# First loads in another order, DRAM stores as operations of their own and a new order of the first eight units, in a Strassen kernel of six cross layers

## The chip, the cores and the metric

The kernel runs on one core of one Trainium2 chip. The metric is the time of one execution on the device in microseconds (us), given as the median of several runs. The profile's own span is shorter than the time (2279.1 us beside 2280.82 us for the run that was profiled). All runs quoted here are fast: no run was more than 1.5% above the fastest of its kernel.

Short names: PE is the matrix engine, PEld its weight loads, DVE the vector engine, ACT the scalar engine, POOL the engine that issues the stores to DRAM here, and SP the engine that issues nearly all the loads. SBUF is the on-chip memory and a PSUM bank a matmul accumulator.

## The reference

```python
B, F, D, L = 16384, 100, 16, 6
Din = min(F * D, 1024)                     # 1024
# x0: (B, Din), ws: (L, Din, Din), bs: (L, Din), all bf16

def reference(x0, ws, bs):
    x = x0
    for l in range(ws.shape[0]):
        proj = jnp.einsum('bd,de->be', x, ws[l]) + bs[l]
        x = x0 * proj + x
    return x
```

Each layer is a matmul of 16384 x 1024 by 1024 x 1024, then a multiply by x0 and an add.

## The kernel before

A *unit* is one layer for one *pair* of 512-row blocks: 16 pairs times 6 layers make 96 units of about 24 us. x is held transposed, features on the partitions, in quadrants: `B11`, `B12`, `B21`, `B22` are (feature half, row half). Each unit's product is made by Strassen's scheme (Winograd's form). DVE makes four sums of x (`T1` to `T4`) and four sums of weight quadrants (combinations 5, 6, 7 and 3), and PE makes seven products `P1` to `P7` instead of eight. From the second pair on, products 5 and 2 are split once more. They need eight more sums of weights (`2i` and `5i`, four quarters each) and six more sums of x (`2t13, 2t2, 2t4, 5t13, 5t2, 5t4`).

Names in the profiles: `wp` are weight quadrants and their sums, in a ring of 16 tiles that are used in turn; `w` is the quadrant w12 (1, w12, 2 and 4 are the four quadrants of a layer's weights); `isum` are the sums 2i and 5i; `x0T` is x0 and `xst` the running x; `T` and `ti` are sums of x; `ev` are products on their way out of PSUM; `Lc` is the DRAM store of the weight sums; `pA` and `pX` are PSUM banks.

The weight sums depend only on the layer. So the first six units make them and *store* them to DRAM (`Lc`), and later units load them. This first pass, about 145 us long, is the only part that the change touches in substance.

```python
isum = [work.tile([P, KH, H], BF16, name=f"isum{i}") for i in range(4)]   # two layers' sums: layer l and l + 2 share
...
def combo(name, w, a, b, o_, deps, u=u, raw=raw):
    def fn():
        t = ring_make(u, w)
        tt(t[:], raw(a)[:], raw(b)[:], o_)                                # DVE
        nc.gpsimd.dma_start(Lc[units[u][1], CIDX[w]]..., t[:])            # its store, at once
    add(name, fn, ...)
...
for X, s in (("2i", isum[2 * (l % 2)]), ("5i", isum[2 * (l % 2) + 1])):
    def icombo(i, fn, rd, wr, ...):       # one quarter; it names only its own quarter
        add(X + i, fn, [f"{X}{l % 2}.{r}" for r in rd] + ..., [f"{X}{l % 2}.{wr}"], [X[0]])
    def save(X=X, s=s, l=l):
        nc.gpsimd.dma_start(Lc[l, CIDX[X]], s[:]...)                      # all four quarters
    icombo("5", ...); icombo("6", ...)
    # "3" and "7" follow; the one that is last by a fixed rule calls save()
```

The order of each engine's instructions is fixed when the program is built. Every operation has a rank (a time in us, relative to its unit's start), a heap takes the lowest rank among the operations whose predecessors are out, and each engine then runs its own in that order. The first eight units have rank tables of their own:

```python
EARLY = [ranks("""P1.3@-.68 P1.1@.19 ... 2i5@-7.88 ... c5@4.62 T1@5.76 ..."""),     # unit 0
 ...
 ranks("""... 2t13@-62.26 2t2@-10.85 T1@-9.38 2t4@-8.25 ...""")]                    # unit 6: second pair, layer 0
...
ttop(X + "t13", t_[:, 0:2], ..., SUB, [src], [X + "t13"])   # "2t13" reads B21, which in unit 6 is x0 of the second pair
ttop(X + "t2", t_[:, 2], q(1, 1), t_[:, 0], SUB, [src, X + "t13"], [X + "t2"])
```

The x0 of the second pair is loaded by two transposing loads (one for each 512 rows), issued in unit 2:

```python
if l == (2 if pr == 0 else 0) and nxt < NPAIR:
    for n in range(2):
        XN = [f"x0.{nxt % 2}.{d}{n}" for d in range(2)]
        def ld(n=n, nxt=nxt):
            nc.sync.dma_start_transpose(out=x0Ts[nxt % 2][:, n], in_=x0[nxt * PR + n * NB:..., :])
        op(base + 23 + n, ld, [], XN)
```

The first loads of all:

```python
for w in ("1", "2"):
    nc.scalar.dma_start(wt[(0, w)][:], w_src(0, w))
nc.scalar.dma_start(b_rows[:], bs...)                  # 12 KB of biases
load_half(nc.scalar, "w12", 0); load_half(nc.scalar, "4", 0)
load_quarter(0, 0); load_quarter(1, 0); load_quarter(0, 1)       # transposing loads of x0, SP
load_half(nc.sync, "w12", 1); load_half(nc.sync, "4", 1)
load_quarter(1, 1)
```

## Time and profile before

| what | value | where it is read |
|---|---|---|
| time | 2281.74 us, 3 runs, 2279.78 to 2283.31 | runs |
| PE busy | 99% of the span | page, part 1 |
| PE on the chain of work that ended last | 96% | page, part 4 |
| 16 matmuls of 128x512 without a gap | 3.45 us (216 ns each) | starts in PE's timeline |
| first real matmul | 9.20 us | PE's timeline |
| idle time of PE after it | 3.7 us in all | PE's waits |

All waits of PE in the kernel before (engine, tile, line, what it waited for: us in total, times, longest):

```profile
PE pX L558 <- DMA b_rows<-in_bs_dram: 3.3, 1, 3.3
PE pX L284 <- DVE T L197: 2.6, 2, 1.5
PE pX L531 <- DVE zeros L528: 1.2, 1, 1.2
PE pX L284 <- DVE wp L197: 0.9, 1, 0.9
PE pX L396 <- DVE ti L197: 0.2, 1, 0.2
```

L284 is the plain matmul, L396 the one of the second split, L197 the helper behind nearly every DVE operation. L558 is a small matmul that transposes the biases, so the first real matmul waits 3.3 us for them (the first quarter of x0, which it needs as well, landed only at 8.95 us). After that there is next to nothing to gain in 2270 us.

### The profile page before, as it was taken

To read this page: it belongs to the slowest core of one execution; us is meant where nothing else is said; L and a number is where in the kernel's file an instruction comes from. 1 tells how busy PE (TensorE), PEld (TensorE's weight loads), DVE (VectorE), ACT (ScalarE), POOL (GpSimd) and SP (SyncE) were. 2 spreads that over 40 slices of the span, in tenths; PEclk is the share of its full clock that TensorE was granted. 3 is DMA by queue.
4 is the path that set the end of the run, shared out by engine and by line. 5 is a ranking of instruction groups with operands and counts; after the bars stand their busy time and mean duration, and the time that the engine had idled before them with its cause. 6 is when DMAs were issued, how large, how long until landed. Compare 5 with 4: busy or idle time off the path is not lost.

```text
span 2279.1 us, 34736 instructions
## 1 busy us (share of the span) xinstructions
PE 2252.4 (99%) x12713; PEld 1263.8 (55%) x12951; DVE 2079.8 (91%) x2326; ACT 1841.2 (81%) x3228; POOL 20.0 (1%) x42
## 2 busy tenths in 40 slices
PE   8999999999999999999999999999999999999998
PEld 3455555555555555555555555555555555555554
DVE  6999999999999999999999999999999999999997
ACT  5678888878888888888888888888888888888887
POOL 1110000000000000000000000000000000000000
PEclk9999999999999999999999999999999999999999
DMA  9869797796977969779697796978969689696872
GB/s 276 241 232 291 271 252 266 211 311 196 247 263 215 302 212 250 258 225 283 215 263 250 226 282 214 262 252 226 284 204 285 233 230 284 195 293 227 240 241 66
DMA packets 625868, 557.01 MB, mean 244 GB/s; under 512 B 397600, under 2 KB 552224, under 8 KB 625696
## 3 DMA queue, kind: packets, MB, share of 16 engines
q1 hardware_dynamic: 617808, 534.05, 79.1%
q0 software_dynamic: 5184, 18.88, 2.1%
q10 hardware_dynamic: 2704, 1.85, 0.3%
q8 instruction: 101, 1.65, 0.3%
q14 instruction: 71, 0.58, 0.1%
HBM read 436.22 MB, written 52.43 MB: 214 GB/s over the span
## 4 chain that ended last, share of the span: by engine, by line
PE 96%; DVE 1%; SPq 1%; issue 1%; DMA 1%; ACT 0%; DVEq 0%; ACTq 0%
PE pA L284 56%; PE pX L396 24%; PE pX L284 16%; DVE ev L197 1%; SPq L534 1%; DMA w<-in_ws_dram 1%; DVE xst L197 0%; ACT ev L293 0%; DVE T L197 0%; DVE isum L197 0%; SPq L547 0%; SPq L245 0%; DVE wp L197 0%; DVE x0T L494 0%; ACT pX L289 0%
## 5 line engine op out<-in xcount | busy, mean ns | idle before, releaser
L284 PEld LDWEIGHTS <-wp 128*128 128x128 bf16 x7904 | 772.3, 98 | 843.0 <-issue 2.9
L284 PE MATMUL pA<-T,wp 128*128 128x512 bf16 x4471 | 1048.6, 379 | 7.2
L293 ACT ACTIVATE ev<-pA,b_all 128x512 bf16<-128x512 f32 x1124 | 706.2, 691 | 212.1 <-PE pA L284 166.3
L396 PEld LDWEIGHTS <-wp 128*128 128x128 bf16 x4984 | 487.0, 98 | 158.3 <-issue 16.1
L197 DVE TENSOR_TENSOR ev<-ev,x0T 128x2048 bf16<-128x2048 bf16 (+2 forms) x484 | 483.2, 1000 | 7.9 <-ACT ev L293 1.3
L197 DVE TENSOR_TENSOR xst<-ev,xst 128x2048 bf16<-128x2048 bf16 x319 | 389.2, 1220 | 18.8 <-DVE ev L197 0.5
L396 PE MATMUL pX<-ti,wp 128*128 128x256 bf16 x2848 | 397.9, 272 | 0.2 <-DVE ti L197 0.2
L197 DVE TENSOR_TENSOR ev<-ev,ev 128x2048 bf16<-128x2048 bf16 (+1 forms) x283 | 343.9, 1215 | 25.5 <-ACT ev L293 7.4
L293 ACT ACTIVATE ev<-pX,b_all 128x512 bf16<-128x512 f32 x412 | 288.9, 706 | 61.4 <-PE pX L284 51.3
L284 PE MATMUL pX<-xst,wp 128*128 128x512 bf16 x1369 | 335.8, 379 | 0.3
L284 PE MATMUL pA<-xst,wp 128*128 128x512 bf16 x1205 | 302.3, 379 | 4.0
L289 ACT COPY pX<-pA 128x512 f32<-128x512 f32 x412 | 256.7, 627 | 39.9 <-PE pA L284 39.9
L289 ACT CAST ev<-pX 128x512 bf16<-128x512 f32 x384 | 225.1, 620 | 52.2 <-ACT ev L293 37.3
L197 DVE TENSOR_TENSOR ev<-iu,ip 128x1024 bf16<-128x1024 bf16 x178 | 122.6, 689 | 120.5 <-ACT iu L289 120.4
L289 ACT COPY pX<-pX 128x512 f32<-128x512 f32 x356 | 208.7, 587 | 8.3
L289 ACT CAST iu<-pX 128x512 bf16<-128x512 f32 x356 | 197.1, 639 | 1.0 <-PE pX L396 0.9
L197 DVE TENSOR_TENSOR T<-xst 128x2048 bf16<-128x2048 bf16 x160 | 194.9, 1218 | 0.3
L197 DVE TENSOR_TENSOR T<-xst,T 128x2048 bf16<-128x2048 bf16 x160 | 194.8, 1218 | 0.2
L396 PE MATMUL pX<-T,wp 128*128 128x256 bf16 x1068 | 160.2, 273 | 0.0
L289 ACT CAST ip<-pX 128x512 bf16<-128x512 f32 x178 | 104.8, 589 | 53.7 <-PE pX L396 53.7
L396 PE MATMUL pX<-xst,wp 128*128 128x256 bf16 x888 | 133.2, 273 | 0.0
L197 DVE TENSOR_TENSOR xst<-ev,x0T 128x2048 bf16<-128x2048 bf16 x64 | 78.3, 1223 | 1.5
(44 smaller groups left out, 621.2 us busy)
## 6 DMA issues: line engine op xcount, KB each, us to landing
wp<-Lc SPq DMA_DIRECT2D x538, 512.0 KB, 4.6
wp<-in_ws_dram SPq DMA_DIRECT2D x285, 512.0 KB, 5.4
out_dram<-x0T SPq DMA_DIRECT2D x30, 1024.0 KB, 8.4
Lc<-wp POOLq DMA_DIRECT2D x24, 512.0 KB, 6.2
Lc<-isum POOLq DMA_DIRECT2D x12, 512.0 KB, 5.5
w<-in_ws_dram SPq DMA_DIRECT2D x5, 512.0 KB, 9.3
wp<-in_ws_dram ACTq DMA_DIRECT2D x2, 512.0 KB, 5.3
out_dram<-x0T SPq DMA_DIRECT2D x2, 512.0 KB, 3.4
```

The source lines that it names most:

```text
L197: nc.vector.tensor_tensor(out=o, in0=a, in1=b, op=op)
L284: nc.tensor.matmul(bank[:], lhsT=wt[(u, w)][:, k, m * P:(m + 1) * P], rhs=rhs[:, k, :], start=(start and k == 0), stop=(k == KH - 1), skip ...
L289: add(name, lambda: nc.scalar.copy(out=dst, in_=src), rd, wr)
L293: add(name, lambda: nc.scalar.activation(out=dst, in_=src, func=IDENT, bias=b_all[:, c:c + 1], scale=1.0), rd, wr)
L396: nc.tensor.matmul(pX[bank][:, m * NQ:(m + 1) * NQ], lhsT=wv[:, k, m * P:(m + 1) * P], rhs=rhs[:, k, :], start=(start and m == 0 and k == ...
L534: nc.sync.dma_start_transpose(out=blk(x0Ts[0], dh, n), in_=x0[n * NB:(n + 1) * NB, dh * H:(dh + 1) * H])
```

## The change

The change does three things. As I read its intent, the first is to start the first unit sooner, the second is to let the scheduler know about the stores, and the third is to refit the order to both.

1. The biases go first on ACT's queue, and the half loads of w12 and 4 all go to SP.
2. A store is an operation of its own, which reads all that it stores. The next writer of the tile has to wait for it.
3. All the rank tables of the first eight units are new.

```diff
+SAVES = ranks("s5@16 s6@17 s7@18 s3@20 s2i@21 s5i@22")
 EARLY = [ranks("""
   ... every table replaced; the two entries that matter below: ...
-2t13@-62.26 2t2@-10.85 T1@-9.38 2t4@-8.25 ...            (unit 6)
+2t13@-153.59 2t2@-151.71 2t4@-29.05 T1@-9.32 ...
-2i5@-14.20 c5@-6.78 ...                                  (unit 4)
+2i5@-22.08 c5@-7.99 T1@5.10 ...
@@
+            def save(w, t, rd, weights=(), l=l):
+                def fn():
+                    nc.gpsimd.dma_start(Lc[l, CIDX[w]]..., t()[:])
+                add("s" + w, fn, rd, (), weights)
@@ combo: ring_make, DVE operation; the store leaves it
+                save(w, lambda raw=raw, w=w: raw(w), [f"w{u}.{w}"], [w])
@@ icombo: the four quarters, in any order that their own inputs allow; f3/f7 with their save() leave
+                save(X, lambda s=s: s, [rn(i) for i in "5637"])
@@ first loads
+    nc.scalar.dma_start(b_rows[:], ...)
     for w in ("1", "2"):
         nc.scalar.dma_start(wt[(0, w)][:], w_src(0, w))
-    nc.scalar.dma_start(b_rows[:], ...)
-    load_half(nc.scalar, "w12", 0)
-    load_half(nc.scalar, "4", 0)
     load_quarter(0, 0)
     load_quarter(1, 0)
     load_quarter(0, 1)
-    load_half(nc.sync, "w12", 1)
-    load_half(nc.sync, "4", 1)
+    for h in range(2):
+        load_half("w12", h)
+        load_half("4", h)
     load_quarter(1, 1)
```

(Cut: the other ranks, the bank of the bias matmul, and plain rewriting.)

**What the second point mends.** In the kernel before, the store of unit 0's `5i` comes with the quarter that the fixed rule calls last, `5i7`, ranked at 54.56 us. Unit 2 shares the tile. Its first quarter, `5i5`, has rank 3.42 in a unit that starts at 48.4, so it is at 51.8, and it names only that one quarter. The order of the built program shows that it is indeed overwritten first (place on the engine, line, operation):

```
DVE  57 L197 TensorTensor isum_102<-wp 128x512      unit 2's 5i5 writes quarter "5" of the tile
DVE  60 L197 TensorTensor isum_102<-wp 128x512      unit 0's 5i7, the last quarter of layer 0
POOL 17 L331 DMACopy Lc<-isum_102 128x2048          the store of layer 0's 5i, after DVE 60
```

The same happens between units 2 and 4. So the kernel before stores a wrong quarter in the `5i` of layers 0 and 2, and passes its comparison with the reference all the same (why it passes was not tested; a wrong x0 in run `e12` below was caught with a relative error of 0.35). The change is thus a correction as well.

## The prediction

> What bounds the kernel now. The matrix engine (PE): busy 2252.4 of 2279.1 us (99%) on the page, and 96% of the chain of waits that ended last. Busy is not rate, so I read starts: four matmuls of 128x512 take 0.86 us, sixteen 3.45 us. From the first real matmul (9.20 us) to the last (2273.2 us) that pace is left at few places only. The list of waits of PE has 1.2 + 3.3 us before the first real matmul, and after it DVE T 2.6 us in two pieces (1.15 us at 17.54, 1.48 us at 44.48), DVE wp 0.9 us at 19.52, DVE ti 0.2 us at 183.57. The change keeps all matmuls and vector work, so it can win at most these 3.7 us and part of the 9 us lead-in.
>
> The pieces of the change.
> 1. First loads. The 12 KB of biases go first on ACT's queue; the four half loads of w12 and 4 all go on SP's queue, after three transposing loads of x0. Before, the first matmul waited for the biases (landed 9.03 us), but the first quarter of x0 landed only at 8.95 us. So that wins 0.1 us. ACT's queue took about 106% of the 16 DMA engines between 8 and 10 us, and the transposes moved 0.05 MB there against 0.48 MB in the next 2 us (DMA view by window). That agrees with the Trainium skill, "DMA: Bandwidth & Descriptors", section "Issuing engines are not separate DMA queues": all queues interleave on the same engines. With the halves gone from there the second and third quarter should land 1 to 2 us earlier (12.64 and 16.17 before), so T1 comes earlier; but the first half of combination 5 comes later (11.3 before, about 16 to 17 after) and becomes the wait of P5. The fourth quarter, which T2 and P6 need, still comes last (20.64 before), and P6 began at 22.12, right after T2. The first unit therefore wins only about 0.4 us.
> 2. Saves as operations. The store of 2i (512 KB, 11.4 to 16.1 us, beside the transposes) moves behind those of 5, 6, 7, 3. The vector engine idled 2.36 us before combination 5 of unit 1, for a w12 that landed at 31.63 us; PE then waited 1.48 us for T1 of unit 1 (43.21 us). After, that chain is about 10.3 us from combination 5 to T1 (before 11.5 us) and w12 should land up to 1 us earlier. About 1.2 us of the 1.48 go away.
> 3. A tile whose save is not issued cannot be reused. Ring and sums have slack. I expect queue waits of SP, no wait of PE.
> 4. New order in units 2 to 7: the vector engine is busy 19 of 20 us there, PE already without gaps: nothing to win, up to a microsecond to lose.
>
> Sum: 0.4 + 1.2 + 0.2 - 0.2 = about 1.6 us. Predicted 2280.1 us, 2276.5 to 2283.5. Within 2%: 98%; faster 1%, slower 1%.
>
> What shows it: PE's wait for T near 44 us shorter than 0.5 us; waits in 16 to 23 us of 1 to 2 us, named combination 5 or T2; w12 of unit 1 landing before 31 us; the first real matmul at 8.5 to 9.2 us; 93 matmuls of 128x512 in 20 us from 60 us on; the page's PE busy time within 3 us of before.
>
> What would make it wrong: the fourth quarter landing well after 21 us, so that P6 waits over 1 us; a save waiting behind an unfinished one on POOL's in-order queue, holding a ring tile so long that unit 3 to 6 lacks weights; a vector order that makes PE wait at a unit's start.

## More of the kernel before

The head of the page of the kernel before:

```profile
span 2279.1 us, 34736 instructions
PE 2252.4 (99%) x12713; PEld 1263.8 (55%) x12951; DVE 2079.8 (91%) x2326; ACT 1841.2 (81%) x3228; POOL 20.0 (1%) x42
```

The trace of this run lacks 238 matmul records: 12713 beside 12951 weight loads, of which there is one for each matmul. PE's busy time can therefore not be compared between two kernels. I compare the starts of the weight loads, which are complete.

What DVE does around 95 us, in unit 3 (start, length, engine, line, operation, out<-in; a bracket would show idle time before it):

```profile
94.78 1.22 DVE L197 TENSOR_TENSOR wp<-wp,w 128x2048 bf16<-128x2048 bf16 x1
...
96.25 0.68 DVE L197 TENSOR_TENSOR ti<-x0T 128x1024 bf16<-128x1024 bf16 x1
96.86 1.22 DVE L197 TENSOR_TENSOR T<-xst 128x2048 bf16<-128x2048 bf16 x1
```

The second line is `2t13` of unit 6, 50 us ahead of its use, put into unit 3. It reads the first 512 rows of the second pair's x0. Their load was issued at 74.06 us and landed 18.3 us later, at 92.37 us (issues of DMA in the window of 72 to 76 us, last number: us from issue to landing):

```profile
x0T<-in_x_dram SPq DMA_TRANSPOSE x1, 18.3
```

So here the load was in 3.9 us before DVE came to its reader. Nobody waited, and no view lists a wait that did not happen.

## The result and the profile after

| kernel | median | runs | ratio to before |
|---|---|---|---|
| before | 2281.14 us | 4, 2279.78 to 2283.31 | |
| changed | 2287.35 us | 4, 2285.37 to 2289.91 | 1.0027, 95% interval 1.001 to 1.0044 |

A ratio is the mean time of one kernel's fast runs over that of the other's fast runs of the same rounds, so it is not quite the ratio of the medians. The change is 0.27% slower, which counts as "same" at 2%, but all four runs lie above the predicted range of 2276.5 to 2283.5 us. The profiled run was the slowest of the four: its span is 9.07 us longer than before's, while the medians differ by 6.2 us.

The head of the page after:

```profile
span 2288.1 us, 34970 instructions
PE 2267.6 (99%) x12951; PEld 1264.2 (55%) x12951; DVE 2080.4 (91%) x2326; ACT 1842.7 (81%) x3228; POOL 19.8 (1%) x42
```

DVE, ACT and PEld do the same work in the same time (here all matmul records are there, so PE's number is no growth). The page alone says nothing. PE's waits after:

```profile
PE pX L286 <- DVE xst L199: 8.3, 2, 7.2
PE pX L286 <- DMA x0T<-in_x_dram: 1.5, 1, 1.5
PE pX L286 <- DVE T L199: 1.3, 1, 1.3
PE pX L518 <- DVE zeros L515: 1.2, 1, 1.2
PE pA L286 <- DMA x0T<-in_x_dram: 0.8, 1, 0.8
...
```

The wait for the biases is gone, and one wait of 7.2 us is new. To see when time was won and lost, I compare the start of the weight load at the same place in PE's order with that of before (us; negative is ahead; my own table from the two traces):

| place (time of before) | 9.2 us | 24 us | 49 us | 86 us | 98 us | 122 us | 580 us | end of span |
|---|---|---|---|---|---|---|---|---|
| changed kernel | -2.38 | -1.88 | -0.83 | -0.83 | +8.54 | +8.54 | +8.31 | +9.07 |

The better start is real (2.4 us at the first real matmul), most of it is gone by 49 us, and one step of 9.37 us between 86 and 98 us makes the whole loss. It is never made up again, as PE has no slack.

DVE's timeline at the step:

```profile
83.42 0.69 DVE L199 TENSOR_TENSOR ev<-ev,x0T 128x1024 bf16<-128x1024 bf16 x1
93.15 0.69 DVE L199 TENSOR_TENSOR ti<-x0T 128x1024 bf16<-128x1024 bf16 x1 [9.04 <-DMA x0T<-in_x_dram]
93.88 0.42 DVE L199 TENSOR_TENSOR ti<-x0T,ti 128x512 bf16<-128x512 bf16 x1
94.22 0.42 DVE L199 TENSOR_TENSOR isum<-wp 128x512 bf16<-128x512 bf16 x1
94.55 1.22 DVE L199 TENSOR_TENSOR xst<-ev,xst 128x2048 bf16<-128x2048 bf16 x1
```

The second line is the same `2t13`. In the new order it has place 78 among DVE's operations instead of 92 (counted from 0), and `2t2`, the other early sum of this x0, has place 79 instead of 144. DVE reaches it at 84.1 us, and its x0 lands only at 93.13 us. DVE runs in order, so everything behind it waits 9.04 us too, among it the `xst` of the fifth line, which has nothing to do with it and which PE needs. The Trainium skill, "TensorE: Matmul & The Clock Gate", section "Architectural detail: the array is 16× 32×32, not 1× 128×128", gives VectorE's queue as strictly first in, first out; this trace agrees, with 9.04 us of idle time and ready work behind it.

The chain of work that ended last, from 84 to 104 us, ties it together (start, length, what). Before, it consists of PE there:

```profile
85.92 3.62 PE pA L284 x16
89.54 6.04 PE pX L284 x28
```

and after, of the load and its readers:

```profile
72.47 20.66 DMA x0T<-in_x_dram
...
93.15 0.70 DVE ti L199
...
94.64 1.14 DVE xst L199
...
95.92 8.20 PE pX L286 x28
```

The wait of PE alone is not the whole step. Windows of before and after (stretch, its length, busy time and count of PE, PEld, DVE, ACT, POOL, then PE's granted clock, the DMA engines' share, GB/s):

```profile
88.50:95.90 7.40, 7.40 (x36) 3.38 (x35) 7.26 (x8) 5.16 (x9) 0.00 (x0) 1.00 1.20 235
95.90:100.00 4.10, 4.05 (x20) 1.86 (x20) 4.10 (x7) 2.54 (x5) 0.53 (x1) 1.00 0.94 198
```

```profile
88.50:95.90 7.40, 0.20 (x1) 0.01 (x1) 2.72 (x5) 0.69 (x2) 0.00 (x0) 0.81 1.10 216
95.90:100.00 4.10, 4.08 (x10) 1.49 (x11) 4.04 (x5) 1.16 (x2) 1.06 (x2) 0.51 0.95 256
```

After the wait PE starts only 10 matmuls in 4.1 us instead of 20, at a granted clock of 0.51. Ten matmuls start 427 ns apart instead of 216 ns, which is 2.1 us. So 7.2 + 2.1 = 9.3 us, the step. The Trainium skill, "TensorE: Matmul & The Clock Gate", section "What's actually happening", says that the clock falls to half after an idle window of about 3.4 us and comes back after as much busy time, with a window that runs freely. The trace agrees: the clock's record goes to half at 93.09 us, 4.4 us after PE ran out of work, and stays there for 6.83 us, about two such windows. In `e2` below a shorter wait was enough; see the last section.

Where did the lead of the start go before that? PE's timeline after:

```profile
6.83 2.75 PE L286 MATMUL pA<-x0T,wp 128*128 128x512 bf16 x12 [0.77 <-DMA x0T<-in_x_dram]
...
11.11 1.89 PE L286 MATMUL pX<-x0T,wp 128*128 128x512 bf16 x8 [1.53 <-DMA x0T<-in_x_dram]
...
38.74 3.61 PE L286 MATMUL pX<-xst,wp 128*128 128x512 bf16 x16 [1.08 <-DVE xst L199]
43.64 2.76 PE L286 MATMUL pX<-T,wp 128*128 128x512 bf16 x12 [1.28 <-DVE T L199]
```

PE begins 2.4 us sooner and then waits 1.5 us for the next quarter of x0, and in unit 1 1.1 us and 1.3 us for DVE. In unit 1 DVE itself is held up by a load. Before:

```profile
31.73 1.23 DVE L197 TENSOR_TENSOR wp<-w,wp 128x2048 bf16<-128x2048 bf16 x1 [2.36 <-DMA w<-in_ws_dram]
```

and after:

```profile
31.50 1.23 DVE L199 TENSOR_TENSOR wp<-w,wp 128x2048 bf16<-128x2048 bf16 x1 [3.50 <-DMA w<-in_ws_dram]
```

This is combination 5 of unit 1, which needs w12. It comes 0.2 us earlier than before, although DVE was free 1.4 us earlier: w12 landed at 31.41 us instead of 31.63 us. The lead ran into a load that had not moved.

### The profile page after: what moved, and what is told of

It is laid out like the page before. It is cut to its first block, busy times and chain, and to the rows that moved or that the text cites. A ratio compares the mean times of both kernels' runs of the same rounds, so it can differ in the third digit from the quotient of the medians.

```text
span 2288.1 us, 34970 instructions
## 1 busy us (share of the span) xinstructions
PE 2267.6 (99%) x12951; PEld 1264.2 (55%) x12951; DVE 2080.4 (91%) x2326; ACT 1842.7 (81%) x3228; POOL 19.8 (1%) x42
## 3 DMA queue, kind: packets, MB, share of 16 engines
q8 instruction: 101, 1.65, 0.3%
## 4 chain that ended last, share of the span: by engine, by line
PE 96%; DMA 1%; DVE 1%; SPq 1%; issue 0%; ACT 0%; DVEq 0%
PE pA L286 56%; PE pX L383 24%; PE pX L286 16%; DMA x0T<-in_x_dram 1%; DVE ev L199 1%; SPq L521 1%; DMA w<-in_ws_dram 1%; DVE xst L199 0%; DVE wp L199 0%; DVE T L199 0%; SPq L530 0%; SPq L247 0%; ACT ev L295 0%; DVE isum L199 0%; DVE x0T L481 0%
## 5 line engine op out<-in xcount | busy, mean ns | idle before, releaser
L286 PE MATMUL pA<-xst,wp 128*128 128x512 bf16 x1280 | 313.5, 379 | 0.0
```

What stands on the lines that cost most here:

```text
L286: nc.tensor.matmul(bank[:], lhsT=wt[(u, w)][:, k, m * P:(m + 1) * P], rhs=rhs[:, k, :], start=(start and k == 0), stop=(k == KH - 1), skip ...
```

## The experiments

The runs are called `e1` to `e14` after the first part of their labels. Theory A: the early place of `2t13` makes the loss, since DVE then waits for the x0 load. Rival B: the stores that are now waited for make it. Rival C: the new first loads make it. Fourteen runs took these apart. "Before" in the tables is the kernel before, run in the same rounds on the same chip.

### Only the two early sums of x put back (e1)

In the changed kernel, two ranks only:

```diff
-2t13@-153.59 2t2@-151.71 2t4@-29.05 T1@-9.32
+2t13@-62.26 2t2@-10.85 2t4@-29.05 T1@-9.32
```

> The changed kernel, but the two vector operations 2t13 and 2t2 of unit 6 (the only ones of the early units that read x0 of the second pair of blocks) go back to the ranks they had before, -62.26 and -10.85. Theory A: the change lost its time in one place, the 9.04 us that the in-order vector engine stood before 2t13 for the second x0 (landed at 93.13 us), which gave PE 7.2 us without work (88.5 to 95.9) and then 2.1 us at half clock (10 matmuls at 427 ns instead of 216). Then this run is at 2287.35 - 9.4 = about 2278 to 2280.5 us, below the kernel before by 0.5 to 3 us, no PE wait over 1 us between 60 and 120 us, PE clock 1.00 in 80 to 100 us. Rival B, the saves as operations made the loads and reuse of tiles late: the wait stays and the time stays at about 2287. Rival C, the rest of the new order is worse as well: the wait goes, but the time stays above 2282.

Measured: median 2282.44 us beside 2280.31 us, ratio 1.0016 (1.0004 to 1.0029); five runs 2282.1 to 2290.1. In the trace (of a run of 2282.44 us) the 9.4 us step is gone: 0.61 us ahead at 86 us, 0.92 us behind at 98 us. A small wait came up instead, of DVE for a store from an `isum` tile, 2.1 us. So A holds for most of the loss, and something is left that varies between runs.

### Only the two early sums of x, in the kernel before (e2)

```diff
-2t13@-62.26 2t2@-10.85 T1@-9.38
+2t13@-153.59 2t2@-151.71 T1@-9.38
```

> The kernel before, with only these two ranks of the change (2t13 at -153.59, 2t2 at -151.71). Theory A: the vector engine meets 2t13 at about 86.5 us and waits for the x0 that landed at 92.4 us before: 5 to 7 us of wait on it, PE without work for 4 to 7 us at the end of P2 of unit 3, 1 to 2 us more at half clock; time 2287 to 2289 us, ratio about 1.003. Rival B and C: within 1 us of before.

Measured: 2287.22 us beside 2280.31 us, ratio 1.0026 (1.0014 to 1.0039), about the whole of the change's loss, with neither its stores nor its loads. DVE's wait from 40 us on:

```profile
DVE ti L197 <- DMA x0T<-in_x_dram: 4.8, 1, 4.8
```

and PE's:

```profile
PE pX L284 <- DVE xst L197: 2.9, 1, 2.9
```

with 3.4 us of half clock behind it. 2.9 us of waiting and 3.4 us at half speed (1.7 us lost) make 4.6 us, and the step in the trace is 4.8 us (0.70 us ahead to 4.09 us behind). The profiled run was the fastest of the five (2285.20 us), so its waits are at the low end.

### Only the new first loads, in the kernel before (e3)

The new first loads, the bias matmul's bank and the rank table of unit 0, without the stores and the other tables.

> The kernel before with the new load order and the new order of unit 0 only. First real matmul at 6.8 us instead of 9.2. My theory D: this lead is given back by 45 us, since the vector operation that makes combination 5 of unit 1 still waits for w12 of unit 1, which lands at about 31.4 us: PE waits in units 0 and 1 rise from 4 to about 5.5 us, and the time is 0 to 1.2 us below before. Rival: the lead stays whole, 2.4 us below before.

Measured: 2283.89 us beside 2280.31 us, ratio 1.0015 (1.0001 to 1.0029). The expected gain did not come. The first real matmul was 1.65 us ahead, and PE was 1.2 us behind at 24 us: the fourth quarter of x0 came late, and the product that needs it, P6, began only after a wait of 1.7 us for T2, with DVE in turn waiting 1.1 us for that quarter. In the changed kernel this wait of P6 is 0.5 us. The difference between the two, apart from the rank tables of later units, is the 2i store of unit 0, which still goes out early here, beside these loads. So the loads lose when they come alone; that the early store is the reason is likely and not shown.

### Only the stores as operations, in the kernel before (e4)

The store operations and their ranks, with the old tables and the old first loads.

> The kernel before with the saves as operations of their own (their ranks as in the change), the old load order and the old order tables. Theory A: no change, within 1 us of before, no new wait of PE. Rival B: a good part of the 6 us appears here, as waits of PE or as a later landing of the second x0 (92.4 us before).

Measured: 2296.24 us beside 2280.31 us, ratio 1.0068 (1.0055 to 1.008), the largest loss of a single part, where no change was expected. DVE's waits from 40 to 150 us:

```profile
DVE isum L198 <- DMA Lc<-isum: 13.2, 3, 5.5
```

and PE's, over the whole trace:

```profile
PE pA L285 <- DVE T L198: 11.5, 3, 4.9
```

The three DVE waits end at 71.0, 101.6 and 131.2 us: each time a quarter of a later layer's `2i` or `5i` wants a tile whose store has not landed. The first and the third store had been issued only just before (at 68.05 and 126.06 us). The second had been issued at 80.40 us and took 21.2 us, beside the transposing loads of x0. PE waits in turn and falls to half clock twice, for 3.4 and 6.8 us. So the correction as such is not free in the old order. What the new rank tables are for becomes plain: they move the first quarters of the sums behind the stores. Rival B is real, but the changed kernel has already paid for it by its order, and its own step is A.

### The store waits of the changed kernel taken away too (e5, e8)

Ranks of `e1`, and in unit 4 one quarter of the sums, `2i5`, from -22.08 to 5.60, behind the store before it.

> The changed kernel with 2t13 and 2t2 of unit 6 late (as in the run before) and, besides, 2i5 of unit 4 late (rank 5.60, after T1 of its unit, instead of -22.08). In the run with only 2t13 and 2t2 late the vector engine stood 2.07 us before this 2i5, for the store of the 2i sums of unit 2 from the same tile, and PE then 1.5 us; two of five runs were 4 and 8 us slower. Theory A2: both are waits of the in-order vector engine for slow DMA at 75 to 95 us, where the transposing load of the second x0 fills the DMA engines; with both moved, no PE wait is left between 50 and 150 us, and the time is 2280 to 2281.5 us in all five runs (within 0.8 us of before). Rival: the spread of the five runs stays 4 us or more.

Measured: 2285.91 us beside 2280.35 us, ratio 1.0025 (1.0012 to 1.0039), but six runs from 2280.33 to 2290.9 us. The profiled run still has a DVE wait of 5.0 us for an `isum` store, at 102.5 us now. This wait was not removed but moved. The experiment missed its aim. PE waited 3.0 us in turn, and its clock stayed at full.

The same `2i5` alone in the changed kernel, with the early `2t13` left in place:

> The changed kernel with only 2i5 of unit 4 late; 2t13 stays early. Theory A2: the longer of the two waits, for x0 (9.04 us), stays whole, so nothing is won: 2285.5 to 2289 us. Rival (the store from the sum tile is the main wait): 2281 to 2283 us.

Measured: 2286.86 us beside 2280.35 us, ratio 1.0026 (1.0014 to 1.0038), as the changed kernel; DVE waits 7.4 us for x0, and the place of `2i5` is not the cause.

### Unit 1's loads in the order of their use (e6)

`e5`, and unit 1's four loads issued in the order 4, w12, 1, 2 instead of 1, 2, 4, w12, with two quarters of 2i in unit 1 ranked behind combinations 5 and 6.

```diff
+            if u == 1:
+                if w == "w12":
+                    for w_ in ("4", "w12", "1", "2"):
+                        nc.sync.dma_start(wt[(1, w_)][:], w_src(1, w_))
+                continue
             nc.sync.dma_start(t[:], w_src(units[u][1], w))
```

> As both late, but the four loads of unit 1 are issued in the order 4, w12, 1, 2 instead of 1, 2, 4, w12, and 2i5, 2i6 of unit 1 go behind combination 6 of unit 1. Theory D: the lead of the new first loads (first real matmul 2 to 2.4 us earlier) is given back because the vector engine stands 3.2 us before combination 5 of unit 1 for w12 (landed at 31.4 to 31.7 us), and PE then waits about 1.0 us for xst and 1.4 us for T1 of unit 1. With w12 landing near 26 us both PE waits go below 0.5 us and the time is 1.5 to 2.5 us under both late, that is 2278 to 2279 us. Rival: the lead is lost to the load of the vector engine (19.9 of 20 us busy), and nothing changes.

Measured: median 2279.51 us beside 2280.35 us, ratio 1.0013 (0.9992 to 1.0034). Four runs are at 2278.05 to 2279.93 us and two at 2290.42 and 2294.43 us, so the mean and the median disagree in sign. In the trace of one of the good runs the lead is 2.88 us from 49 to 98 us, where the changed kernel had 0.83 us, and the two waits of unit 1 are gone. DVE's wait for w12 is gone as well. So I take w12's place in the queue as the reason of the second loss; the two quarters of 2i were moved along with it, and neither was tried alone. What makes two of six runs slow is still open here.

### Zeros to keep the clock up (e7)

In the changed kernel, 24 matmuls of zeros (which add nothing to their bank) between P1 and P2 of unit 3, where PE waits.

> The changed kernel with 24 matmuls of zeros (5.2 us, they add nothing to the sums) between P1 and P2 of unit 3, where PE otherwise has no work for 7.2 us. Theory H: PE's clock halved because it was idle too long (4.5 us from its last matmul to the drop), which cost 10 matmuls at 427 ns, 2.1 us. With the zeros no half clock shows between 80 and 105 us and the time is 1 to 2.5 us under the changed kernel: 2284.5 to 2286.5 us. Rival: the drop has another cause; half clock and time stay.

Measured: 2286.02 us beside 2280.59 us, ratio 1.0025 (1.001 to 1.004). The clock stayed at full and no matmul was slow (window after the wait, columns as above):

```profile
93.00:97.00 4.00, 3.95 (x19) 1.67 (x18) 3.86 (x5) 2.12 (x4) 0.00 (x0) 1.00 0.98 295
```

The time is 1.3 us under the 2287.35 us of the changed kernel, in other rounds. But in this profile DVE's wait for x0 was 5.0 us and not 9.0 us, so part of that can be a shorter wait. And here the zeros outlasted it: the `xst` that P2 needs was done at 91.32 us, but the zeros held PE until 93.28 us, so they cost about 1.8 us themselves. Without them PE would have stood idle for some 3.2 us, and the 3.0 us of `e5` left the clock at full. That the slow matmuls go with the half clock is shown by the clock's record; that the zeros prevented it in this run, and how much of the 2.1 us they mend in a median, is not.

### Other tiles for the sums of two layers (e9)

`e4`, with the sums of units 2 and 3 in a buffer that is idle until unit 6 (the second pair's x), so that no quarter waits for a store of the layer two before:

```diff
-            for X, s in (("2i", isum[2 * (l % 2)]), ("5i", isum[2 * (l % 2) + 1])):
+            held = [f"xs.1.{a_}{b_}" for a_, b_ in QD] if l in (2, 3) else []
+            sums = [blk(xsts[1], l % 2, n) for n in range(2)] if held else isum[2 * (l % 2):2 * (l % 2) + 2]
```

> The saves as operations with the old orders (that run took 2296.2 us, 16 us over before, with four waits of the vector engine before a write of a sum tile for the store from it, 14.2 us), but the sums of units 2 and 3 lie in the xst buffers of the second pair, which lie idle until unit 6, so that no sum tile is written again within two units of its store. Theory E: the 16 us are the wait of the tile's next use for its store, PE stalls and half clock behind it included; without that need the time is 2279 to 2282 us, and the vector engine has no wait on a store of sums over 0.5 us. Rival F, the saves' later place or the traffic costs the time: it stays above 2290 us.

Measured: 2287.81 us beside 2280.35 us, ratio 1.0031 (1.0019 to 1.0043). The waits for stores are gone, and so is half of `e4`'s loss, but a wait of another kind has come in their place:

```profile
DVE ti L198 <- DMA x0T<-in_x_dram: 7.9, 1, 7.9
```

That is `2t13` again, in its old place. x0 lands at 103.45 us here instead of 92.37 us; I take it that the stores, no longer spread out by waits, go out closer to the transposing loads.

### The second pair's x0 loaded one unit earlier (e10)

In the changed kernel, with its early `2t13` in the same place of DVE's order (its rank had to be made later for that, -73.80 instead of -153.59, as it would otherwise have gone out still sooner):

```diff
-        if l == (2 if pr == 0 else 0) and nxt < NPAIR:
+        if l == (1 if pr == 0 else 0) and nxt < NPAIR:
```

> The changed kernel, with one thing moved: the two transposing loads of the second x0 are issued in unit 1 (about 47 us) instead of unit 2 (72.5 us). 2t13 and 2t2 keep their place in the vector engine's order. Theory A: the loss is the early 2t13 meeting the late x0; with x0 landed by 70 us the 9 us wait and the half clock go, and so do the waits for stores of sums at 85 to 105 us that the runs with 2t13 moved still showed. 2279 to 2282 us, spread of the runs under 3 us. Rival: the transposes stretch the stores wherever they are, and another wait of 3 us or more appears between 47 and 70 us: time above 2284.

Measured: 2280.43 us beside 2280.59 us, ratio 1.0002 (0.9989 to 1.0014), with runs within 1.6 us. The place of `2t13`, the stores and the first loads are those of the changed kernel, and the whole loss is gone. All that DVE still waits for from 40 to 150 us:

```profile
DVE ev L199 <- ACT ev L295: 0.7, 2, 0.5
```

and the load that `2t13` reads lands 13.3 us after its issue (48.52 to 61.77 us), where it took 18.3 us before and 20.7 us after; both loads of this run (issues from 48 to 57 us, median):

```profile
x0T<-in_x_dram SPq DMA_TRANSPOSE x2, 11.4
```

The store wait of `e1` is gone as well, though the store and its reader stand where they stood, and so is that of `e6` in `e11` below, which is `e6` with the load moved. This says that the stores landed late in those runs because they went beside the transposes. That the slow runs of `e5` and `e6` come from this is an inference: only one run of each was profiled, and the small spread here (and in `e11`, 1.4 us) is what speaks for it.

### The same load without the transpose (e12)

In the changed kernel, the second pair's x0 by plain loads of the same bytes. The result is wrong (relative error 0.35).

> The changed kernel, but the second x0 is loaded by plain loads of the same bytes from the same place in the queue; the result is wrong on purpose. Theory G: it is the transposing load beside the stores to DRAM that is slow ([...]1 MB took 20.7 us), not the volume. Plain, 1 MB lands in 5 to 9 us, before about 84 us, 2t13 does not wait over 1 us, and the time is 2279 to 2282 us. Rival: the DMA engines are just full there; x0 lands after 88 us, 2t13 waits 4 us or more and the time stays above 2284.

Measured: 2280.69 us beside 2280.59 us, ratio 1.0 (0.9986 to 1.0013). The first 512 rows are in at 82.58 us, before DVE gets to `2t13` at 84.16 us, and DVE does not wait. DMA by queue (q1 holds SP's loads, q0 POOL's stores; packets, MB, share of the 16 engines' time). The changed kernel, from 80 to 93 us:

```profile
q1 hardware_dynamic: 2004, 0.50, 81.4%
q0 software_dynamic: 287, 1.04, 38.3%
```

and this run, from 73 to 88 us:

```profile
q1 hardware_dynamic: 2510, 3.55, 73.0%
q0 software_dynamic: 432, 1.57, 25.7%
```

Plain loads and stores together moved 5.12 MB in 15 us (341 GB/s), transposing loads and stores 1.54 MB in 13 us (119 GB/s), with the engines taken for most of the time in both (in the changed kernel they stand mostly idle from 88.4 to 89.8 us). The kernel before has each kind alone: transposes from 94 to 96 us,

```profile
q1 hardware_dynamic: 2267, 0.58, 127.5%
```

which is 0.58 MB in 2 us (290 GB/s), and stores from 70 to 72 us, 0.43 MB (215 GB/s, with the queue running dry at about half of it). So neither is slow alone. In the records a 256-byte packet of a transpose takes 18 ns alone, and beside the stores, from 80 to 93 us of the changed kernel, 86 ns on average and up to 1.57 us. A 4 KB packet of a store takes 159 ns alone and also beside the plain loads, but beside the transposes 311 ns on average and up to 2.64 us. It is the two side by side, but not at a fixed rate: the kernel before, from 81 to 92 us, moved 2.61 MB of both kinds (237 GB/s), most of it stores, while its x0 still took 18.3 us. What inside the DMA engines makes this is open. The plain loads also move packets of 2 KB instead of 256 bytes, so whether the transposing or the small packets matter is not separated. And a store can land late beside plain loads too: one of `isum` took 10.0 us here, against 17.9 us in the changed kernel and 5.8 us in `e10`.

### The best of both (e11)

`e6` with the x0 load in unit 1:

```diff
-        if l == (2 if pr == 0 else 0) and nxt < NPAIR:
+        if l == (1 if pr == 0 else 0) and nxt < NPAIR:
...
-                op(base + 23 + n, ld, [], XN)
+                op(base + (10 if pr == 0 else 23) + n, ld, [], XN)
```

> A try at the best version: as the run with both late and the loads of unit 1 reordered (2278 to 2280 us in four of six runs, 2290 and 2294 in two), with the load of the second x0 issued in unit 1, at about 33 us. The two slow runs should go, because no load of x0 meets the stores of units 2 and 3: all runs 2277.5 to 2280 us, ratio 0.999. Rival: the weights of units 2 and 3 or the stores of unit 1 are now late and PE waits over 2 us between 45 and 75 us: 2281 us or more.

Measured: 2278.07 us beside 2280.59 us, ratio 0.9991 (0.9978 to 1.0004). All five runs (2277.94 to 2279.35 us) lie below all nine of before (2279.6 us at the lowest), but the interval just includes 1, so this is better than the changed kernel for certain, and better than before by about 0.1%, if at all. The lead of 3.5 us holds from 49 us to the place at 580 us, and 2.8 us are left at the end of the span. PE's waits are those of the start:

```profile
PE pX L291 <- DMA x0T<-in_x_dram: 1.4, 1, 1.4
PE pX L523 <- DVE zeros L520: 1.2, 1, 1.2
PE pA L291 <- DMA x0T<-in_x_dram: 1.0, 1, 1.0
...
```

### What the correct stores cost in the old order (e13, e14)

`e4` and `e9`, each with the x0 load in unit 1 and nothing else.

> The saves as operations with the old orders (2296.2 us), with the second x0 loaded in unit 1. It shows how much of the 16 us is the wait of a sum tile's next use for its store in its own right, with stores landing in 3 to 7 us as elsewhere, and how much came from the stores and transposes in each other's way. Theory E: most is the wait in its own right, since the next use stands right behind the store in the old order: three waits of the vector engine for stores of sums stay (3 to 5 us each), 2287 to 2293 us. Rival G alone: with the transposes away the stores land in time, 2280 to 2284 us.

> As the run before, and besides the sums of units 2 and 3 lie in idle buffers, as in the run that had this alone (2287.8 us, one wait of 7.9 us for the second x0). With neither the tile's reuse nor the transposes beside the stores, theories E and G together leave nothing of the 16 us: 2279 to 2282 us, no wait of the vector engine for a store or for x0 over 1 us after 30 us. If it stays above 2284 us, a third cost of the saves' new place has been missed.

Measured: `e13` 2301.75 us beside 2280.61 us, ratio 1.0093 (1.0076 to 1.0109), the slowest of all and slower than either theory expected, and `e14` 2279.78 us, ratio 0.9998 (0.9983 to 1.0013). DVE's waits from 40 to 150 us, first `e13`, then `e14`:

```profile
DVE isum L198 <- DMA Lc<-isum: 18.0, 2, 12.4
```

```profile
DVE ev L198 <- ACT ev L294: 1.7, 5, 0.6
```

In `e13` the moved transposes (50 to 80 us, over 21 us for each load) now meet a store that a DVE operation is waiting for. It was issued at 67.74 us, landed 12.05 us later, and DVE lost 12.4 us in one piece. So moving the load is no remedy by itself: it only moves the collision, and whether it costs anything depends on who waits for the slowed store. In `e14` nobody waits for a store, and the load is early enough for `2t13`. The correct stores are then as fast as the incorrect ones of before. Only both together take `e4`'s loss away; `e9` alone takes half of it, and `e13` adds to it.

## Why the prediction was wrong

The size of change that the prediction gave, -1.6 us against before, was wrong in sign: the medians differ by +6.2 us. Point by point:

- **"4. New order in units 2 to 7: the vector engine is busy 19 of 20 us there, PE already without gaps: nothing to win, up to a microsecond to lose."** This is the step that failed. The order lost 9.4 us at one place in the trace (7.2 us of PE's wait and 2.1 us of half clock), and about the whole difference of the medians: 6.9 us when it alone is put into the kernel before (`e2`). I read from DVE's busy share and from PE's missing gaps that the order has little to lose. Neither says how close an operation stands to the landing of its data, and on the in-order queue that decides. I ought to have looked for operations that moved forward past their data. The order of the built program, which I had, shows `2t13` going from place 92 to 78, and before's trace shows that its load came in only 3.9 us before it was used.
- **"3. ... Ring and sums have slack. I expect queue waits of SP, no wait of PE."** Wrong for the stores as such: alone, they cost 16 us (`e4`), since the sums' tiles have no slack in the old order. In the changed kernel this did not show in the profile, as the new tables had moved the quarters; with the wait for x0 gone, `e1` still had one of 2.1 us for a store.
- **Items 1 and 2, the sum of 1.6 us.** In item 1 the mechanism was right (the quarters of x0 land sooner when the half loads leave) and the size was off, as the first quarter was left out: it landed at 6.79 us instead of 8.95 us. The first real matmul came at 6.83 us and not at 8.5 to 9.2 us: the win in the first unit was 2.4 us at its first matmul and 1.9 us at its end, and not 0.4 us. In item 2 the step from the later 2i store to an earlier w12 failed. In unit 1 the term of +1.2 us was in fact -1.05 us (a lead of 1.88 us at 36 us and of 0.83 us at 49 us). "w12 of unit 1 landing before 31 us" failed with 31.41 us, and "PE's wait for T near 44 us shorter than 0.5 us" with 1.28 us. Together 0.83 us were won by 49 us. `e6` points to w12's place in the queue as the reason.
- **What would make it wrong.** "... a vector order that makes PE wait at a unit's start" names the right kind of fault, but the loss was allowed "up to a microsecond" in item 4. The fourth quarter of x0 was not late: P6 waited 0.48 us.
- **Right:** what bounds the kernel, that at most a few us could be won, and that the class would be "same". The page's PE busy time was not a fit test: before's trace lacked 238 records.

The prediction cites the Trainium skill, "DMA: Bandwidth & Descriptors", section "Issuing engines are not separate DMA queues", for all queues interleaving on the same engines. The runs agree that SP's loads and POOL's stores share them (q1 and q0 above), and show that sharing is not a matter of bytes alone.

## What to carry to other kernels

On an in-order engine, an operation that is moved forward has to be checked against the landing time of what it reads: here it cost its own wait and that of all the ready work behind it, and then the matrix engine's clock. Before a reorder is judged, list the operations that moved forward, with the slack in the old trace between the landing and the first use; here a slack of 3.9 us behind a load of 18 us was used up when its reader came 12.1 us sooner (84.11 instead of 96.25 us). And look whether transposing loads and stores to DRAM run side by side where somebody waits for either of them: in this kernel one moved load of x0 took the loss away (`e10`), and the same move in another order made it larger (`e13`).

## What the Trainium skill lacked or had wrong

- "DMA: Bandwidth & Descriptors", section "Latency and other measured facts", gives DMA_TRANSPOSE an effective 261 GB/s with a non-contiguous middle dimension and about 350 to 400 GB/s in the contiguous case. Alone, the transposing loads moved 290 GB/s here (0.58 MB in 2 us), between the two. The page lacks that transposes and stores to DRAM can slow each other: together 119 GB/s (1.54 MB in 13 us) in the changed kernel, against 341 GB/s for plain loads and the same kind of stores.
- The same page, section "Rules for kernel authors": "A transpose next to ordinary DMAs needs nothing". That is about correctness, and no run here contradicts it there. In time it needs care: the load of x0 that the sum reads took 20.7 us beside the stores and 13.3 us when moved by one unit, and a store of 512 KB that a DVE operation waited for took 12.05 us (`e13`).
- No page says how much longer a store to DRAM holds the tile that it reads when transposes run beside it. Here the median from issue to landing of a 512 KB store of a sum was 5.5 us over the first 200 us of the kernel before, and 17.9 us for one issued beside the transposes in the changed kernel.
- "TensorE: Matmul & The Clock Gate", section "What's actually happening", has the clock fall after at least one idle window of about 3.4 us. The changed kernel agrees (half clock 4.4 us after PE ran dry, 427 ns instead of 216 ns for a matmul), and half-clock stretches were 3.4, 6.8 and 13.7 us. But in `e2` a wait of PE of 2.9 us was enough, while one of 3.0 us in `e5` left the clock at full. So a gap shorter than a window can halve the clock, and need not; that it depends on where the gap falls in the window would fit, but was not tested.
